# V's first projections in another order in the head of an attention and gated-MLP kernel

## The chip, the cores and the metric

The kernel runs on one NeuronCore of a Trainium2 chip. The metric is the device time of one execution in microseconds (us). A core has TensorE (PE; its weight loads are PEld), VectorE (DVE), ScalarE (ACT), GpSimd (POOL) and SyncE (SP); here SyncE mostly issues transfers.

## The reference, cut to what matters

x has 2048 rows of D = 640; all of it is bf16. There are 32 heads of 20, a causal window of W = 256, and an MLP of F = 1536.

```python
xn = layernorm(x)
q, k, v = split(xn @ wqkv)                 # 32 heads of 20
p = softmax(where(mask, q @ k.T * 20**-0.5, -1e9))   # 0 <= i - j < 256
a = (p @ v) @ wo
g, u = xn @ w_gate, xn @ w_up
out = x + a + (sigmoid(g) * u) @ w_down
```

## The kernel before, in words

The rows are worked off in four chunks of 512 (`NCH`, `CW`), each of four blocks of 128 rows (`SBC`). For a chunk the kernel needs xnT, the normalised rows transposed, so that D lies on the partitions as DC = 5 pieces of 128. Q and K are projected with the weights as the stationary operand (`proj_block`, L263), copied to bf16, written to a scratch in DRAM and read back spread over partitions. V is projected with xnT as the stationary operand, as it is wanted with rows on the partitions. Scores, softmax and the product with V are done in steps of up to eight pairs of 64-row blocks. Between these steps a planner (`class Fill`) pulls other PE work: the MLP's gate and up sums (`g_gu`, L411 and L420), the next chunk's projections, and the output. Its list is fixed when the program is built.

The change lies in the head, which does chunk 0 before the planner starts. Its order is written out by hand, and every engine carries out its own list in that order. PE transposes the normalised rows of a block itself (`transpose_rows`, L230: five transposes into a PSUM tile of the pool `ps_h`, then one or two copies to xnT at L231). The blocks come in the order 0, 1, 3, 2. Blocks 0 and 3 have their mean and variance from VectorE (`ln_half`, `ln_mv`, `norm`), blocks 1 and 2 from ScalarE (`mean_act`, `root_act`) with the last step on VectorE (`norm_act`, L647 and L648). V's sum of block s and half h (320 of 640 columns) is five matmuls, one for each piece of D (`project_v`, L301). It lies in a PSUM buffer of the pool `ps_d` (four buffers, taken in turn) or of `ps_h`. Two casts of 64 rows each bring it to the tile v (`copy_v`, L309).

Before the first transposes PE does ten matmuls on constant ones (L196), which nothing reads. All loads of the head go through SyncE's queue in the order written: block 0, 1 and 3 of x, the first half of V's weights (all five pieces, columns 0 to 319, 400 KB), block 2 of x, the other half of V's weights, Q's weights, K's weights (800 KB each), and the first quarters of w_gate and w_up (L156, 480 KB each). x's next chunk (L115) needs the buffer of chunk 0, so it is issued when all four blocks are normalised. After that GpSimd makes a small copy of it (`landed`, L700), which holds back two transfers that clear the scratch (L153). The Q and K projection of chunk 0 follows the head's last V sum on PE, and the planner's work follows that.

Of the kernel before, what the change touches and what calls it, by code (L numbers as in the profile page):

```python
# [9 lines left out]
P = 128  # L10
S = 2048
D = 640
# [3 lines left out]
DC = D // P  # L16
FC = F // P
CW = 512
# [6 lines left out]
HALF = 320  # L25
FS = 768
# [10 lines left out]
FP32 = mybir.dt.float32  # L37
# [29 lines left out]
def kernel(  # L67
# [11 lines left out]
    nc = tc.nc  # L79
# [23 lines left out]
    ps_h = banks.enter_context(tc.tile_pool(name="ps_h", bufs=4, space=bass.MemoryType.PSUM))  # L103
# [6 lines left out]
    def load_x(c):  # L110
        t = xp.tile([P, SBC, D], BF16, name="xc")
        xc[c] = t
        rows = x2[c * CW:(c + 1) * CW, :].rearrange("(a n t) d -> a t n d", a=SBC, n=SBC)
        for a in range(SBC):
            nc.sync.dma_start(out=t[32 * a:32 * a + 32], in_=rows[a])  # L115

    wqkv = const.tile([P, DC, 3 * D], BF16, name="wqkv")
    wqkv_r = A_wqkv.rearrange("(c p) n -> p c n", p=P)
    wg = [const.tile([P, DC, FS], BF16, name=f"wg{k}") for k in range(F // FS)]
    wu = [const.tile([P, DC, FS], BF16, name=f"wu{k}") for k in range(F // FS)]  # L120
# [3 lines left out]
    ones = nc.const_aps.tensor(1.0, [P, CW], BF16)  # L124
    def load_wqkv(part):
        nc.sync.dma_start(out=wqkv[:, :, part * D:(part + 1) * D],
                          in_=wqkv_r[:, :, part * D:(part + 1) * D])
# [3 lines left out]
    def load_rows(s, queue):  # L131
        queue.dma_start(out=xc[0][:, s, :], in_=xr[:, s, :])  # L132

    def load_v(hf):
        a = 2 * D + hf * HALF
        nc.sync.dma_start(out=wqkv[:, :, a:a + HALF], in_=wqkv_r[:, :, a:a + HALF])

    load_rows(0, nc.sync)
    load_rows(1, nc.sync)
    load_rows(3, nc.sync)  # L140
    load_v(0)
    load_rows(2, nc.sync)
    load_v(1)
    load_wqkv(0)
    load_wqkv(1)

# [8 lines left out]
    def load_gu(t, w, k, lo=0, hi=FS):  # L155
        nc.sync.dma_start(out=t[k][:, :, lo:hi],  # L156
                          in_=w.rearrange("(c p) f -> p c f", p=P)[:, :, k * FS + lo:k * FS + hi])

    load_gu(wg, B_w_gate, 0, 0, FS // 2)
    load_gu(wu, B_w_up, 0, 0, FS // 2)  # L160
    
    def load_second():
        load_gu(wg, B_w_gate, 1, FS // 2)
# [26 lines left out]
    nc.gpsimd.memset(eps, EPS)  # L190
    scr = const.tile([P, 1], FP32, name="scr")
    nc.scalar.activation(out=scr, in_=eps, func=SQRT)
    for n in (6, 4):
        ps = ps_d.tile([P, CW], FP32, name="pwarm", tag="d")
        for k in range(n):
            nc.tensor.matmul(ps, lhsT=ones[:, 0:P], rhs=ones, start=(k == 0), stop=(k == n - 1))  # L196


    xnT = {}
# [2 lines left out]
    def ln_half(c, s, a, stats=None):  # L202
        if a == 0:
            stats = lnp.tile([P, 2, nc.vector.BN_STATS_DIM], FP32, name="stats")
        nc.vector.bn_stats(out=stats[:, a, :], in_=xc[c][:, s, a * HALF:(a + 1) * HALF])
        return stats

    def ln_mv(stats, mv=None):
        if mv is None:
            mv = lnp.tile([P, nc.vector.BN_AGGR_DIM], FP32, name="mv")  # L210
        nc.vector.bn_aggr(out=mv, in_=stats)
        return mv
# [14 lines left out]
    def transpose_rows(s, copy, lo=0, hi=DC):  # L227
        pt = ps_h.tile([P, DC, P], BF16, name="pt", tag="pt")
        for d in range(lo, hi):
            nc.tensor.transpose(pt[:, d, :], xns[0, s][:, d * P:(d + 1) * P], ident)  # L230
        copy(out=xnT[0][:, s, lo:hi, :], in_=pt[:, lo:hi, :])  # L231
# [65 lines left out]
    def project_v(c, s, hf, lo=0, hi=DC, ps=None):  # L297
        if ps is None:
            ps = ps_d.tile([P, CW], FP32, name="pv", tag="d")
        for d in range(lo, hi):  # L300
            nc.tensor.matmul(ps[:, 0:HALF], lhsT=xnT[c][:, s, d, :],  # L301
                             rhs=wqkv[:, d, 2 * D + hf * HALF:2 * D + (hf + 1) * HALF],
                             start=(d == 0), stop=(d == DC - 1))
        return ps

    def copy_v(c, s, hf, ps, copy, blocks=(0, 1)):
        v4 = vt[c * SBC + s][:, :, 0:16 * VW].rearrange("p b (h d) -> p b h d", d=VW)
        for b in blocks:
            copy(out=v4[U * hf:U * hf + U, b, :, 0:DH],  # L309
                 in_=ps[U * b:U * b + U, 0:HALF].rearrange("p (h d) -> p h d", d=DH))  # L310

    def proj_v(c, s, hf, copy):
        copy_v(c, s, hf, project_v(c, s, hf), copy)
# [175 lines left out]
    def scores(c, step):  # L489
        pt = pp.tile([P, HG, NK, U], BF16, name="pT")  # L490
        ps = ps_s.tile([P, HG, CW], FP32, name="ps")
        for pr, k, q, n, col in step["pieces"]:
            kc, kb = divmod(c * NK + k, NK)
            half, r = divmod(pr, 2)
            for side in range(2):
                for i in range(HG):
                    nc.tensor.matmul(  # L497
                        ps[side * U:(side + 1) * U, i, col * U:(col + n) * U],
                        lhsT=qk["k", kc, half][32 * i:32 * i + DH, 2 * r + side, kb * U:(kb + 1) * U],
                        rhs=qk["q", c, half][32 * i:32 * i + DH, 2 * r + side, q * U:(q + n) * U],  # L500
                        start=True, stop=True)
        used = max(col + n for *_, n, col in step["pieces"])
        nc.scalar.activation(out=pt[:, :, 0:used, :], in_=ps[:, :, 0:used * U], func=EXP, scale=SCALE)  # L503

        if step["one"]:
            col, n, sign = step["one"]
            for side in range(2):
                select(pt[side * U:(side + 1) * U, :, col:col + n, :], n, sign)

        def masks():  # L510
            col, kind, n = step["pair"]
            part = pt[:, :, col:col + n, :].rearrange("p h n u -> p h (n u)")
            limit = keep[:, kind:kind + n, :].rearrange("p n u -> p (n u)").unsqueeze(1)
            nc.vector.tensor_tensor(out=part, in0=part, in1=limit.to_broadcast([P, HG, n * U]), op=MIN)  # L514

        return pt, masks
# [102 lines left out]
    def root(mv):  # L619
        r = lnp.tile([P, 1], FP32, name="rstd")  # L620
        nc.scalar.activation(out=r, in_=mv[:, 1:2], func=SQRT, bias=eps)
        return r
# [23 lines left out]
    def norm_act(s, xn, neg, r):  # L646
        nc.vector.reciprocal(r, r)  # L647
        nc.vector.tensor_scalar(out=xn, in0=xc[0][:, s, :], scalar1=neg[:, 0:1],  # L648
                                scalar2=r[:, 0:1], op0=ADD, op1=MULT)
# [10 lines left out]
    act, dve = nc.scalar.copy, nc.vector.tensor_copy  # L660
# [5 lines left out]
    stats3 = ln_half(0, 3, 0)  # L666
    for lo, hi in ((0, 3), (3, DC)):
        transpose_rows(0, act, lo, hi)
    norm_act(1, xn1, neg1, r1)
    mv3 = ln_mv(ln_half(0, 3, 1, stats3))  # L670
    transpose_rows(1, dve)
    v00 = project_v(0, 0, 0)
    r3 = root(mv3)
    xn2, neg2 = mean_act(2)
    r2 = root_act(2, xn2, neg2)
# [2 lines left out]
    copy_v(0, 0, 0, v00, dve, (0,))  # L678
    transpose_rows(3, dve)
    copy_v(0, 0, 0, v00, dve, (1,))  # L680
    v01 = project_v(0, 0, 1)
    norm_act(2, xn2, neg2, r2)
    copy_v(0, 1, 0, v10, act)
    v30 = project_v(0, 3, 0)
    copy_v(0, 0, 1, v01, act)
    v11 = project_v(0, 1, 1, ps=ps_h.tile([P, CW], FP32, name="pvh", tag="pt"))
    copy_v(0, 3, 0, v30, act)
    transpose_rows(2, dve)
    v31 = project_v(0, 3, 1, ps=ps_h.tile([P, CW], FP32, name="pvh", tag="pt"))
    copy_v(0, 1, 1, v11, act)  # L690
    copy_v(0, 3, 1, v31, dve)
    proj_v(0, 2, 0, act)
    proj_v(0, 2, 1, dve)
    nc.scalar.activation(out=scr, in_=neghalf[:, 0:1], func=EXP)
    banks.close()
    ps_s = banks.enter_context(tc.tile_pool(name="ps_s", bufs=1, space=bass.MemoryType.PSUM))
    load_x(1)
    load_gu(wg, B_w_gate, 0, FS // 2)
    landed = const.tile([P, 2], BF16, name="landed")
    nc.gpsimd.tensor_copy(out=landed, in_=xc[1][:, 0, 0:2])  # L700
# [55 lines left out]
    for t, (c, pr, k, step) in enumerate(todo):  # L756
# [10 lines left out]
        pt, masks = scores(c, step)  # L767
# [74 lines left out]
```

## Time and profile before

| | us |
|---|---|
| median of 3 runs | 309.64 |
| lowest and highest | 309.34 and 315.12 |
| the profiled execution's own time | 310.91 |
| its span, first to last instruction | 309.2 |
| V's first matmul in that execution | 7.01 |
| first Q/K matmul | 14.70 |
| first gate matmul (L411) | 25.49 |
| first up matmul (L420) | 26.57 |

Times within the profile count from the span's start. A row of a timeline has its start, its length, the engine, the line, the operation, the tiles written and read, the shape and the count; the length of several is from the first one's start to the last one's end. In square brackets is how long the engine had been idle and who ended that. A matmul's length has its drain in it, so back-to-back matmuls overlap. The chain of waits is followed back from the last instruction and shows start, length and who held the end; there the matmuls do not overlap, and their lengths are shares of the chain.

### The profile page before, as it was taken

Reading aid. Unit: us, or ns where it says so; the run is one execution under the profiler, and the core shown is the slowest. Engines: PE = TensorE matmul, PEld = TensorE weight load, DVE = VectorE, ACT = ScalarE, POOL = GpSimd, SP = SyncE. Lnnn points to the kernel's source line nnn. Section 1 sums busy time; section 2 is a strip of 40 time slices with the busy share of each in tenths; the row PEclk is TensorE's granted clock in tenths of the full one; section 3 lists DMA queues with packets and bytes.
Section 4 is the critical chain, followed back from the end, with each engine's and each line's share of the span. In section 5 each row is a group of like instructions: output and inputs, shape, how many; then the busy total and the mean of one; then the engine's idle time right before and its main releaser. Section 6 shows DMA issues by size and latency. Waiting matters only on the chain.

```text
span 309.2 us, 10136 instructions
## 1 busy us (share of the span) xinstructions
PE 305.0 (99%) x4431; PEld 169.0 (55%) x4431; DVE 186.3 (60%) x373; ACT 192.8 (62%) x184; POOL 83.8 (27%) x183
## 2 busy tenths in 40 slices
PE   8999999999999999999999999999999999999996
PEld 3654445564556655644456655654446665444774
DVE  4577548678992679577564557355383626465523
ACT  6823686888764657777674656877676466768000
POOL 5011124554314133332223132331313232231100
PEclk9999999999999999999999999999999999999999
DMA  7996939879937322540252112560000210000301
GB/s 213 344 265 192 346 90 274 226 239 310 211 125 176 119 73 87 174 137 11 78 127 63 47 58 88 167 203 2 2 2 3 66 45 23 2 2 2 87 22 64
DMA packets 35756, 36.86 MB, mean 119 GB/s; under 512 B 2944, under 2 KB 35456, under 8 KB 35712
## 3 DMA queue, kind: packets, MB, share of 16 engines
q1 hardware_dynamic: 34304, 33.84, 37.1%
q0 software_dynamic: 544, 1.61, 1.7%
q10 hardware_dynamic: 864, 0.77, 0.9%
q8 instruction: 34, 0.56, 0.8%
q14 instruction: 10, 0.08, 0.1%
HBM read 25.59 MB, written 11.44 MB: 120 GB/s over the span
## 4 chain that ended last, share of the span: by engine, by line
PE 97%; DMA 1%; ACT 1%; DVE 0%; SPq 0%; issue 0%
PE pg L411 18%; PE y L434 17%; PE pu L420 17%; PE pqk L263 14%; PE ps L497 9%; PE y L441 7%; PE acc L530 6%; PE pv L321 6%; PE pv L301 2%; DMA xc<-in_A_x_dram 1%; PE pt L230 0%; PE pvh L301 0%; ACT turn L637 0%; ACT turn L642 0%; DVE turn L648 0%; SPq L132 0%
## 5 line engine op out<-in xcount | busy, mean ns | idle before, releaser
L503 ACT ACTIVATE pT<-ps 128x2048 bf16<-128x2048 f32 x76 | 141.1, 1856 | 61.8 <-PE ps L497 56.2
L486 POOL TENSOR_SCALAR_AFFINE_SELECT pT<-pT 64x256 bf16<-64x256 bf16 (+1 forms) x120 | 67.7, 564 | 183.4 <-ACT pT L503 132.7
L411 PE MATMUL pg<-xnT,wg 128*128 128x512 bf16 x240 | 59.9, 380 | 0.0
L420 PE MATMUL pu<-xnT,wu 128*128 128x512 bf16 x240 | 59.8, 380 | 0.0
L424 DVE SCALAR_TENSOR_TENSOR h<-th,pu 128x512 bf16<-128x512 f32 x48 | 32.8, 683 | 44.4 <-ACT th L414 25.9
L434 PE MATMUL y<-wd,h 128*128 128x320 bf16 (+2 forms) x396 | 57.0, 296 | 0.0
L263 PE MATMUL pqk<-xnT,wqkv 128*128 128x512 bf16 x200 | 45.9, 381 | 0.0
L434 PEld LDWEIGHTS <-h 128*128 128x128 bf16 x396 | 36.7, 98 | 16.3 <-issue 2.5
L514 DVE TENSOR_TENSOR pT<-pT,keep 128x512 bf16<-128x512 bf16 (+1 forms) x76 | 35.3, 465 | 13.9 <-ACT pT L503 13.0
L414 ACT ACTIVATE th<-pg 128x512 f32<-128x512 f32 x48 | 28.6, 595 | 14.8 <-PE pg L411 14.3
L420 PEld LDWEIGHTS <-wu 128*128 128x128 bf16 x240 | 22.3, 98 | 27.6 <-issue 2.0
L411 PEld LDWEIGHTS <-wg 128*128 128x128 bf16 x240 | 21.7, 98 | 27.0 <-issue 3.6
L263 PEld LDWEIGHTS <-wqkv 128*128 128x128 bf16 x200 | 22.5, 119 | 19.2 <-issue 1.8
L497 PE MATMUL ps<-qT,kT 20*64 20x320 bf16 (+4 forms) x1440 | 32.2, 261 | 0.0
L445 DVE SCALAR_TENSOR_TENSOR rows<-y,rows 128x320 bf16<-128x320 f32 x30 | 14.6, 489 | 24.9 <-PE y L441 24.8
L541 DVE STREAM_TRANSPOSE t<-acc 128x512 f32<-128x512 f32 x32 | 20.9, 692 | 12.1 <-PE acc L530 12.1
L497 PEld LDWEIGHTS <-kT 20*64 20x64 bf16 x1440 | 13.1, 103 | 23.0 <-issue 21.9
L441 PE MATMUL y<-wo,oc 128*128 128x320 bf16 (+2 forms) x165 | 24.2, 295 | 0.0
L530 PEld LDWEIGHTS <-v 64*32 64x32 bf16 x1440 | 17.0, 92 | 6.7 <-issue 1.8
L530 PE MATMUL acc<-pT,v 64*32 64x320 bf16 (+4 forms) x1440 | 20.0, 253 | 0.0
L441 PEld LDWEIGHTS <-oc 128*128 128x128 bf16 x165 | 15.5, 98 | 6.5 <-issue 1.0
L321 PE MATMUL pv<-wqkv,xnT 128*64 128x320 bf16 x240 | 17.4, 300 | 0.0
(61 smaller groups left out, 177.4 us busy)
## 6 DMA issues: line engine op xcount, KB each, us to landing
qT<-sq SPq DMA_DIRECT2D x16, 256.0 KB, 4.6
kT<-sk SPq DMA_DIRECT2D x16, 256.0 KB, 5.0
xc<-in_A_x_dram SPq DMA_DIRECT2D x16, 160.0 KB, 4.0
sq<-st SPq DMA_DIRECT2D x20, 128.0 KB, 3.5
sk<-st SPq DMA_DIRECT2D x20, 128.0 KB, 2.6
out_dram<-rows SPq DMA_DIRECT2D x15, 160.0 KB, 1.8
wg<-in_B_w_gate_dram SPq DMA_DIRECT2D x4, 480.0 KB, 7.3
wu<-in_B_w_up_dram SPq DMA_DIRECT2D x4, 480.0 KB, 8.2
```

What stands on the lines that cost most here:

```text
L263: nc.tensor.matmul(ps, lhsT=wt[:, m, :], rhs=xnT[c][:, :, d, :], start=(d == 0), stop=(d == DC - 1))
L321: nc.tensor.matmul(ps[hf * U:(hf + 1) * U, 0:HALF], lhsT=xnT[c][:, s, d, rows], rhs=wqkv[:, d, 2 * D + hf * HALF:2 * D + (hf + 1) * HALF], ...
L411: nc.tensor.matmul(pg, lhsT=part(wg, d, f), rhs=xnT[c][:, :, d, :], start=(d == 0), stop=(d == DC - 1))
L420: nc.tensor.matmul(pu, lhsT=part(wu, d, f), rhs=xnT[c][:, :, d, :], start=(d == 0), stop=(d == DC - 1))
L424: nc.vector.scalar_tensor_tensor(out=h, in0=th, scalar=1.0, in1=pu, op0=ADD, op1=MULT)
L434: nc.tensor.matmul(y[:, 0:cut[1] - cut[0]], lhsT=ht[c, f][:, s * P:(s + 1) * P], rhs=wd[:, f, cut[0]:cut[1]], start=(f == 0), stop=False)
L441: nc.tensor.matmul(y[:, 0:cut[1] - cut[0]], lhsT=oc[c, m][:, s * P:(s + 1) * P], rhs=wo[:, m, cut[0]:cut[1]], start=False, stop=(m == DC - 1))
L486: nc.gpsimd.affine_select(out=part, in_=part, pattern=pattern, compare_op=GE, fill=0.0, base=-1 if sign > 0 else 0, channel_multiplier=sign)
L497: nc.tensor.matmul(ps[side * U:(side + 1) * U, i, col * U:(col + n) * U], lhsT=qk["k", kc, half][32 * i:32 * i + DH, 2 * r + side, kb * U: ...
L503: nc.scalar.activation(out=pt[:, :, 0:used, :], in_=ps[:, :, 0:used * U], func=EXP, scale=SCALE)
L514: nc.vector.tensor_tensor(out=part, in0=part, in1=limit.to_broadcast([P, HG, n * U]), op=MIN)
L530: nc.tensor.matmul(accs[side][32 * i:32 * i + 32, q * U:(q + n) * U], lhsT=vt[sb][rows, b, at:at + 32], rhs=pt[rows, i, col:col + n, :], s ...
```

## The change

V's weights are loaded by pieces of the contraction over all 640 columns: pieces 0 to 2 (480 KB) and pieces 3 and 4 (320 KB). On PE the first three matmuls of V's sum of block 0, half 0 stand between the transposes of block 0 and those of block 1, behind one more matmul on ones with 256 columns. Both halves of block 0 are summed ahead of block 1's first half, each in two parts; block 1's second half comes between the transposes of blocks 3 and 2. Casts change places between ScalarE and VectorE. The load of w_up's first quarter is issued behind x's next chunk.

```diff
-    def load_v(hf):
-        a = 2 * D + hf * HALF
-        nc.sync.dma_start(out=wqkv[:, :, a:a + HALF], in_=wqkv_r[:, :, a:a + HALF])
+    def load_v(lo, hi):
+        nc.sync.dma_start(out=wqkv[:, lo:hi, 2 * D:], in_=wqkv_r[:, lo:hi, 2 * D:])
...
-    load_v(0)
+    load_v(0, 3)
     load_rows(2, nc.sync)
-    load_v(1)
+    load_v(3, DC)
...
     load_gu(wg, B_w_gate, 0, 0, FS // 2)
-    load_gu(wu, B_w_up, 0, 0, FS // 2)
...
-    for n in (6, 4):
+    def warm(n, cols):
         ps = ps_d.tile([P, CW], FP32, name="pwarm", tag="d")
         for k in range(n):
-            nc.tensor.matmul(ps, lhsT=ones[:, 0:P], rhs=ones, start=(k == 0), stop=(k == n - 1))
+            nc.tensor.matmul(ps[:, 0:cols], lhsT=ones[:, 0:P], rhs=ones[:, 0:cols], start=(k == 0), stop=(k == n - 1))
+
+    warm(6, CW)
+    warm(4, CW)
...
     for lo, hi in ((0, 3), (3, DC)):
         transpose_rows(0, act, lo, hi)
+    warm(1, CW // 2)
+    v00 = project_v(0, 0, 0, 0, 3)
     norm_act(1, xn1, neg1, r1)
     mv3 = ln_mv(ln_half(0, 3, 1, stats3))
     transpose_rows(1, dve)
-    v00 = project_v(0, 0, 0)
+    v01 = project_v(0, 0, 1, 0, 3)
+    project_v(0, 0, 0, 3, DC, v00)
+    project_v(0, 0, 1, 3, DC, v01)
     r3 = root(mv3)
...
     transpose_rows(3, dve)
     copy_v(0, 0, 0, v00, dve, (1,))
-    v01 = project_v(0, 0, 1)
+    v11 = project_v(0, 1, 1)
     norm_act(2, xn2, neg2, r2)
+    copy_v(0, 0, 1, v01, act)
+    v30 = project_v(0, 3, 0, ps=ps_h.tile([P, CW], FP32, name="pvh", tag="pt"))
     copy_v(0, 1, 0, v10, act)
-    v30 = project_v(0, 3, 0)
-    copy_v(0, 0, 1, v01, act)
-    v11 = project_v(0, 1, 1, ps=ps_h.tile([P, CW], FP32, name="pvh", tag="pt"))
-    copy_v(0, 3, 0, v30, act)
     transpose_rows(2, dve)
     v31 = project_v(0, 3, 1, ps=ps_h.tile([P, CW], FP32, name="pvh", tag="pt"))
     copy_v(0, 1, 1, v11, act)
-    copy_v(0, 3, 1, v31, dve)
-    proj_v(0, 2, 0, act)
-    proj_v(0, 2, 1, dve)
+    copy_v(0, 3, 0, v30, dve)
+    copy_v(0, 3, 1, v31, act)
+    proj_v(0, 2, 0, dve)
+    proj_v(0, 2, 1, act)
...
     load_x(1)
+    load_gu(wu, B_w_up, 0, 0, FS // 2)
     load_gu(wg, B_w_gate, 0, FS // 2)
```

## The prediction

> **What bounds the kernel now.** I read the page's first two parts, then the chain of waits of the head, then the head's rows on PE, VectorE and SyncE's queue, and last the landing times of the loads.
>
> ```profile
> span 309.2 us, 10136 instructions
> ...
> PE 305.0 (99%) x4431; PEld 169.0 (55%) x4431; DVE 186.3 (60%) x373; ACT 192.8 (62%) x184; POOL 83.8 (27%) x183
> ```
>
> TensorE has work during 99% of the span and the chain that ended last lies on it for 97%. Behind the head comes one PE stream whose order the change leaves alone, so the time moves by as much as the first Q/K matmul (at 14.70 us) moves, unless a load comes late further on. The chain of waits of the head:
>
> ```profile
> 6.00 0.46 DVE turn L648
> 6.46 0.05 issue
> 6.50 0.71 PE pt L230 x5
> 7.22 2.67 PE pv L301 x10
> 9.88 0.46 PE pt L230 x5
> 10.35 1.44 PE pv L301 x10
> 11.79 0.68 PE pvh L301 x5
> 12.46 0.28 PE pt L230 x5
> 12.74 0.68 PE pvh L301 x5
> 13.42 1.44 PE pv L301 x10
> ```
>
> I call the five transposes of block s Ts, and V's sum of block s and half h Vsh. The order is T0, T1, V00, V10, T3, V01, V30, V11, T2, V31, V20, V21. A V matmul takes 2.67/10 = 0.267 us up to 9.9 and 0.68/5 = 0.136 after; five transposes take 0.53 and 0.28. So PE's rate doubles near 10.1, inside T3; the row PEclk reads full speed from the start, and the rate has to be taken from the matmuls. PE's own rows:
>
> ```profile
> 5.36 0.71 PE L230 MATMUL pt<-ident,turn 128*128 128x128 bf16 x5
> 6.50 0.71 PE L230 MATMUL pt<-ident,turn 128*128 128x128 bf16 x5 [0.43 <-DVE turn L648]
> 7.01 2.87 PE L301 MATMUL pv<-wqkv,xnT 128*128 128x320 bf16 x10
> 9.68 0.67 PE L230 MATMUL pt<-ident,turn 128*128 128x128 bf16 x5
> 10.18 1.60 PE L301 MATMUL pv<-wqkv,xnT 128*128 128x320 bf16 x10
> ```
>
> T0 is streamed by 5.36 + 5 x 0.107 = 5.90; T1 waits for block 1's normalised rows until 6.50. This 0.60 hole (0.43 from the end of the last result) is the only large one. VectorE between T3 and T2:
>
> ```profile
> 10.38 0.49 DVE L231 COPY xnT<-pt 128x640 bf16<-128x640 bf16 x1 [1.31 <-PE pt L230]
> 10.91 0.49 DVE L309 CAST v<-pv 64x320 bf16<-64x320 f32 x1
> 11.32 0.15 DVE L647 RECIPROCAL rstd<-rstd 128x1 f32<-128x1 f32 x1
> 11.51 0.45 DVE L648 TENSOR_SCALAR turn<-xc,neg,rstd 128x640 bf16<-128x640 bf16 x1
> ```
>
> T2 needs the last of these: 11.96, and 0.05 to issue, 12.01. PE came to T2 at 12.30, so this chain had 0.29 to spare, and no more.
>
> **The change, part by part.** Times on this execution's clock.
>
> *V00's first part before T1.* T0 ends its stream at 5.90; the added 256-column matmul takes half of a warm-up matmul (ten started from 0.85 to 4.64, 0.42 each), 0.21, to 6.11. It lies in the hole; without the hole it would cost its 0.21. V00 over chunks 0 to 2 needs two things. ScalarE's copy of chunks 0 to 2 runs from 5.90 to 6.38. The weights: before, the first V load was issued at 2.19 and landed 4.1 later, at 6.3; now it carries 480 KB instead of 400, in runs of 1280 bytes instead of 640. Per engine that is 24 packets for 40; I take the same landing, 6.3. Bounds: before 6.38 nothing is gained, as the copy ends then; late, block 2's rows, issued behind it, landed at 2.67 + 4.0 = 6.7. So it starts at 6.50, bounds 6.45 and 6.77. T1 was ready at 6.50, and is now queued behind three matmuls of 0.267: it starts at 7.30. What waits for T1: VectorE's copy (now 8.07 to 8.56), then block 3's norm (7.85 + 0.45 before, now to 9.23), then T3, which PE reaches at 10.58. These 0.80 are not lost, as V00 is three matmuls shorter later. This edit costs 0, bounds -0.05 and +0.27.
>
> *V01 ahead of V10.* After T1 (to 7.83) come three matmuls of V01 to 8.63, two of V00 to 9.17, two of V01 to 9.70, then V10. The second weight load is needed at 8.63. Its landing has no row; it lies between block 2's rows, 6.7, and Q's weights, 3.71 + 6.8 = 10.5. Q's 800 KB should take what K's took, 12.8 - 10.5 = 2.3, so V's old 400 KB were there by 8.2, and the new 320 KB by about 6.7 + 0.8 x 1.5 = 7.9 (estimate). Cost 0; the late end, 8.2, is also in time. With the clock doubling at 10.1, V10 ends at 10.58 and T3's stream at 10.86. Before, T3's ended at 10.18 with three V sums still to come before T2; now two, V11 and V30.
>
> *Two sums instead of three between T3 and T2.* T3's stream end to T2 ready was 12.01 - 10.18 = 1.83, all on VectorE and in an unchanged order (copy, cast, reciprocal, norm). Before, PE filled it with 3 x 0.68 and a 0.07 wait for the copy of T3, 2.11. Now it has 2 x 0.68 + 0.07 = 1.43. The stall is 1.83 - 1.43 = 0.40, before T2. So T2 starts at 10.86 + 1.83 = 12.69 against 12.30. Bounds: 0, if T3 got as much earlier as VectorE then needs; and 0.68, a whole sum, if the spare 0.29 vanished as well. I take 0.40, as all its terms are rows of this very chain.
>
> *Copies shared anew.* ScalarE still makes ten half casts (0.86 a pair) and VectorE six. V21's cast moves to ScalarE and V20's to VectorE; the PSUM buffer of V21 is wanted by the fourth Q/K sum, 3 x 1.08 after the first, and its cast is done 1.1 after V21. ScalarE's table load (1.28) then ends some 0.5 later, while its next work was at 21.38. Cost 0. T2 to Q/K stays 14.70 - 12.30 = 2.40.
>
> *w_up's first quarter, 480 KB, moved.* It leaves SyncE's row at 6.31 (2.02 of issuing) and goes behind the four loads of x's second chunk and ahead of a w_gate quarter and ten Q/K stores. x's loads wait for block 2's norm, now 12.64, and take 1.76 of issuing; w_up and w_gate 0.43 each end at about 15.4, and the first store waits for VectorE until 17.1. The bytes before the stores are the same. x lands about 480 KB, or 1.5 us, earlier; w_up then lands after x at 17 to 19, where its first user was at 26.57. GpSimd's clearing transfers wait for x (19.59 before) and start 3 earlier: 768 KB more beside w_up and w_gate, 2.2 at the 344 or so GB/s of the page's second slice. Even with all of that w_up is there by 21. Cost 0, cover 5 us or more; an up-weight later than 26.6 would cost its lateness.
>
> **Sum:** 0 + 0 + 0.40 + 0 + 0 = +0.40 on the profiled execution's 310.91 us (span 309.2, 1.7 around it), so 311.3. The median of the runs shown, 309.64, is 1.27 lower. An execution whose rate doubled before T0 would fit: with fast matmuls T1 stays at 6.50, V00 at 6.78, V10 waits for T1's copy to 7.67, T3 8.35 to 8.63, then V01, V30, V11 end at 10.75, and Q/K starts at 10.75 + 2.40 = 13.15, 1.55 less. In that case the change gives: V00's first part 6.37, T1 6.78, V01's first part 7.06, V00's rest waits for the second load from 7.47 to some 7.77, T3 ends at 9.27, T2 at 11.10, Q/K at 13.50: +0.35. Either way about +0.4; on the median **310.0 us**.
>
> [...]
>
> **The rivals.**
> A, faster: the rate doubles at 6.7, because PE's hole shrinks from 0.60 to 0.39 and sums stand on both sides of T1. It decides on whether these 0.21 are enough for the hole not to count. Then T1 is at 7.04, V00's rest at 7.8, V10 at 8.27, T3 ends at 9.23, T2 starts at 11.06, Q/K at 13.46: -1.24, 308.4 on the median. For it: the hole lies 3.6 us ahead of the doubling, and the median run fits an early doubling. Against: 0.85 to 5.3 had no hole, and the rate did not double.
> B, the weights gate T1: the larger first load lands with block 2's rows at 6.7, V00 starts at 6.77 and all behind it with it: +0.27 more, +0.67, 310.3. For it: 80 KB more ahead of its end. Against: 24 packets an engine for 40.
> C, neutral: T3 comes early enough, or VectorE's chain is short enough, that the stall is covered: 0, 309.6. Against: the chain has 0.29 of slack and loses a cover of 0.68.
> D, slower: the second weight load lands after 8.63, say at 8.9, PE gets a hole there, and the doubling comes 3.6 behind it, at 12.5. Then V10 ends at 11.30, T3's stream at 11.83, and T2 starts 1.83 later, at 13.7: +1.4, 311.0. It decides at a landing of 8.63. For it: this landing has no row. Against: 7.9 by the bytes, and at the latest 8.2.
>
> **How the numbers follow.** The forecast's chance is 0.5, A 0.14, B 0.12, C 0.12, D 0.09, and 0.03 for a late load or a disturbance of 2% (6.2 us, about what a measurement of this kernel can tell from no change: its runs lay between 309.34 and 315.12). The range runs from A, 308.3, past D to the forecast from the profiled execution's own time, 311.3 with 0.1 to spare; the forecast's own is 309.7 to 310.4. All five cases are within 2%: faster 0.01, same 0.96, slower 0.03.
>
> **What would show it.** In the changed profile: V00's first matmul at 6.4 to 6.8 and T1 behind it at 7.2 to 7.6 on the slow clock; no wait before V00's rest; PE idle 0.3 to 0.5 before T2, put down to VectorE's norm; x's loads landed near 17; first Q/K matmul 0.4 later than in the same clock state. A matmul rate that doubles before 9 us in the changed kernel's record would not by itself make the forecast wrong, as executions may differ in it; what would is PE reaching T2 after the norm, a second hole before V00's rest on the slow clock, or a load that PE waits for behind the head.

## The result, and the profile after

| | before | changed |
|---|---|---|
| median of 18 runs | 309.4 us | 311.25 us |
| lowest and highest | 309.15 and 315.12 | 310.0 and 313.74 |
| ratio to before | | 1.0061, 95% interval 1.0043 to 1.0078 |
| the profiled execution's time, span | 310.91, 309.2 | 310.0, 308.3 |
| first Q/K matmul in it | 14.70 | 13.81 |

The changed kernel is slower by 0.6%, clear of noise and inside 2%. Another series of runs (r_after below), beside its own executions of before, gave 310.31 against 309.49 (ratio 1.0029, 0.9996 to 1.0062), an interval that just reaches 1. The single profile seems to say the opposite: the changed kernel's span is 0.9 shorter. That is the state of PE's clock in the two executions. The page of the profile after:

```profile
span 308.3 us, 10137 instructions
...
PE 303.7 (99%) x4432; PEld 168.2 (55%) x4432; DVE 186.3 (60%) x373; ACT 192.7 (62%) x184; POOL 84.4 (27%) x183
```

PE's rows of the changed head:

```profile
5.31 0.72 PE L231 MATMUL pt<-ident,turn 128*128 128x128 bf16 x5
5.82 0.42 PE L194 MATMUL pwarm<-const-bfloat16-1.0 128*128 128x256 bf16 x1
6.82 0.57 PE L302 MATMUL pv<-wqkv,xnT 128*128 128x320 bf16 x3 [0.58 <-DMA wqkv<-in_A_wqkv_dram]
7.22 0.44 PE L231 MATMUL pt<-ident,turn 128*128 128x128 bf16 x5
7.50 1.96 PE L302 MATMUL pv<-wqkv,xnT 128*128 128x320 bf16 x12
9.30 0.44 PE L231 MATMUL pt<-ident,turn 128*128 128x128 bf16 x5
9.58 0.84 PE L302 MATMUL pv<-wqkv,xnT 128*128 128x320 bf16 x5
10.33 0.85 PE L302 MATMUL pvh<-wqkv,xnT 128*128 128x320 bf16 x5
11.40 0.45 PE L231 MATMUL pt<-ident,turn 128*128 128x128 bf16 x5 [0.22 <-DVE turn L649]
```

Five transposes take 0.72 at 5.31 and 0.44 at 7.22: the rate doubled between 6.0 and 6.8 here, and at 10.1 in the profile of before. So the two profiles can't be subtracted. What can be compared is each wait: PE stood before V00 for the weights (a wait that before did not have) and before T2 for block 2's norm. Behind the head nothing changed: from the first Q/K matmul to the end it is 309.21 - 14.70 = 294.51 before and 308.30 - 13.81 = 294.49 after. In twelve of the thirteen profiles of this document it lies between 294.4 and 294.9; the thirteenth, of e_v00a, comes at the end.

The comparable profile of before is that of e_wu below: PE's list is that of before, its rate doubled ahead of T0, and its Q/K projection begins at 13.24 in an execution of 309.46. Against it the changed kernel's profiled execution lost 0.57 in the head and 310.0 - 309.46 = 0.54 in time.

### The profile page after: what moved, and what is told of

It reads as the page before. It is cut to its first block, busy times and chain, and to the rows that moved or that the text cites. A ratio compares the mean times of both kernels' runs of the same rounds, so it can differ in the third digit from the quotient of the medians.

```text
span 308.3 us, 10137 instructions
## 1 busy us (share of the span) xinstructions
PE 303.7 (99%) x4432; PEld 168.2 (55%) x4432; DVE 186.3 (60%) x373; ACT 192.7 (62%) x184; POOL 84.4 (27%) x183
## 4 chain that ended last, share of the span: by engine, by line
PE 96%; ACT 1%; DVE 1%; DMA 1%; issue 0%; SPq 0%
PE pg L412 18%; PE y L435 18%; PE pu L421 17%; PE pqk L264 15%; PE ps L498 9%; PE y L442 7%; PE acc L531 6%; PE pv L322 6%; PE pv L302 1%; DMA xc<-in_A_x_dram 1%; ACT turn L638 1%; DVE turn L649 0%; ACT turn L643 0%; PE pt L231 0%; PE pvh L302 0%
## 5 line engine op out<-in xcount | busy, mean ns | idle before, releaser
L415 ACT ACTIVATE th<-pg 128x512 f32<-128x512 f32 x48 | 28.5, 595 | 14.7 <-PE pg L412 14.3
```

## The experiments

In the tables "low clock" counts executions whose mean granted clock was 0.997 or less. One stretch of 3.4 us at half rate, as e_nowarm's profile below shows it from 7.4 to 10.8, is 1.7 of 310 us; that execution reads 0.994. Before had 4 of 109 such executions in the four series of the experiments; the changed kernel had 9 of 30, counting the 18 executions of its result and the 12 of r_after. The kernels of one series were run beside the same executions of before; each of the four series ran on another chip, so counts and medians of different series are compared with care.

| first series (before 309.49) | median | fastest | ratio, interval | low clock |
|---|---|---|---|---|
| r_after | 310.31 | 309.74 | 1.0029, 0.9996 to 1.0062 | 4 of 12 |
| e_wu | 309.50 | 309.18 | 0.9981, 0.9954 to 1.0007 | 1 of 12 |
| e_nowu | 310.39 | 309.70 | 1.0015, 0.9987 to 1.0043 | 2 of 12 |
| e_v10 | 310.42 | 309.62 | 1.0019, 0.9991 to 1.0048 | 4 of 12 |

**r_after**: the changed kernel again.

> The changed kernel again, for a second profile. Theory 1 (clock): the changed head has three holes on PE (before V00, before V00's rest, before T2), which cost some 0.65 us in an execution whose matmul rate doubles by 6.8 us, and beyond that they make the rate double later or fall back in a part of the executions, 1.7 us for each stretch of 3.4 at half rate; so times from 310.0 to 313, median 311.2, and a profile that either looks like the first one or shows V's matmuls at 0.267 us past 7 us. Theory 2 (queue): the moved load of w_up puts later transfers in each other's way, and PE waits somewhere behind 14 us; the same times, but the profile shows a wait of PE behind the head.

The profile looked like the first: V00 at 6.71, the first Q/K matmul at 13.71, no wait behind the head. The times fell into three heaps, 309.74 to 310.02, 310.6 to 310.68 and 312.01 to 312.73; the last heap is the four with a low clock. Nothing for theory 2. The median that theory 1 gave, 311.2, was missed.

**e_wu**: before, with only the moved load of w_up.

```diff
     load_gu(wg, B_w_gate, 0, 0, FS // 2)
-    load_gu(wu, B_w_up, 0, 0, FS // 2)
...
     load_x(1)
+    load_gu(wu, B_w_up, 0, 0, FS // 2)
     load_gu(wg, B_w_gate, 0, FS // 2)
```

> The kernel before with the load of w_up's first quarter alone moved behind x's next chunk. Theory 1 (clock): the PE order and its holes are those of before, so 309.4 within 0.2, with a spread as narrow as before's. Theory 2 (queue): 310.5 to 311.3 with the wide spread.

309.50, as before: the move costs nothing. Its rows on PE:

```profile
5.37 0.45 PE L229 MATMUL pt<-ident,turn 128*128 128x128 bf16 x5 [0.75 <-DVE turn L223]
6.51 0.45 PE L229 MATMUL pt<-ident,turn 128*128 128x128 bf16 x5 [0.69 <-DVE turn L647]
6.80 1.60 PE L300 MATMUL pv<-wqkv,xnT 128*128 128x320 bf16 x10
8.24 0.44 PE L229 MATMUL pt<-ident,turn 128*128 128x128 bf16 x5
8.79 1.53 PE L300 MATMUL pv<-wqkv,xnT 128*128 128x320 bf16 x10
...
13.24 1.03 PE L262 MATMUL pqk<-xnT,wqkv 128*128 128x512 bf16 x4
```

This is before's order with the early clock: T1 at 6.51, right behind it V00 at 6.80, and only one small wait later, 8.52 to 8.79, for the second half of V's weights.

**e_nowu**: the reverse, the changed kernel with that load at its old place.

> The changed kernel with the load of w_up's first quarter at its old place. Theory 1 (clock): 311.0 to 311.4, spread from 310 to 313, as PE's holes stay. Theory 2 (queue): 309.8 to 310.1 with a narrow spread.

310.39 beside r_after's 310.31: the load is not the cause. The forecast of 311.0 to 311.4 took the median of the result for the whole, and missed.

**e_v10**: the changed kernel with V10 behind T3.

```diff
-    v10 = project_v(0, 1, 0)
     copy_v(0, 0, 0, v00, dve, (0,))
     transpose_rows(3, dve)
     copy_v(0, 0, 0, v00, dve, (1,))
+    v10 = project_v(0, 1, 0)
     v11 = project_v(0, 1, 1)
```

> The changed kernel with V10 moved from ahead of T3 to behind it, so that three V sums lie between T3 and T2 again, as before. Theory 1 (clock): the hole before T2 is gone, 0.2 to 0.4 less than the changed kernel in the same clock state, and fewer executions at half rate if that hole is one of those that matter: 310.3 to 311.0. Theory 2 (queue): 0.2 to 0.4 less from the head and the same spread as the changed kernel.

```profile
6.74 0.57 PE L302 MATMUL pv<-wqkv,xnT 128*128 128x320 bf16 x3 [0.85 <-DMA wqkv<-in_A_wqkv_dram]
...
11.05 0.44 PE L231 MATMUL pt<-ident,turn 128*128 128x128 bf16 x5
...
13.45 0.81 PE L264 MATMUL pqk<-xnT,wqkv 128*128 128x512 bf16 x3
```

T2 has no wait, and the Q/K projection begins at 13.45 against 13.71 in r_after, whose V00 began within 0.03 of it: the stall before T2 is worth 0.26. The low clocks stayed (4 of 12), so they do not need that stall.

| second series (before 309.46) | median | fastest | ratio, interval | low clock |
|---|---|---|---|---|
| e_fill | 310.55 | 309.80 | 1.0027, 1.0009 to 1.0044 | 0 of 12 |
| e_nowarm | 311.82 | 309.98 | 1.0049, 1.0028 to 1.0071 | 5 of 11 |
| e_v00a | 310.17 | 309.56 | 1.0027, 1.0007 to 1.0047 | 1 of 12 |
| e_bfill | 309.55 | 309.12 | 0.9993, 0.9967 to 1.0019 | 0 of 12 |

**e_nowarm**: the changed kernel without the line `warm(1, CW // 2)`.

> The changed kernel without the added matmul on ones behind T0, so the hole before V00 is 0.1 to 0.2 us longer. Theory 1a: executions with a mean clock near 0.995 are as frequent as in the changed kernel or more, 4 to 8 in 12, median 310.5 to 312. Theory 1b: 3 or 4 in 12. In both the fastest stay at 309.7 to 310.0, as the matmul lies in the hole.

This profile caught the clock falling back. PE's rows, and the granted clock in three stretches of it (columns: stretch, length, busy time and count of PE, PEld, DVE, ACT, POOL, then PEclk, DMA share, GB/s):

```profile
5.36 0.45 PE L231 MATMUL pt<-ident,turn 128*128 128x128 bf16 x5 [0.64 <-DVE turn L225]
7.10 0.68 PE L302 MATMUL pv<-wqkv,xnT 128*128 128x320 bf16 x3 [1.29 <-DMA wqkv<-in_A_wqkv_dram]
7.57 0.74 PE L231 MATMUL pt<-ident,turn 128*128 128x128 bf16 x5
8.11 3.14 PE L302 MATMUL pv<-wqkv,xnT 128*128 128x320 bf16 x12
11.08 0.44 PE L231 MATMUL pt<-ident,turn 128*128 128x128 bf16 x5
```

```profile
4.10:7.40 3.30, 1.37 (x11) 0.70 (x10) 2.43 (x8) 2.63 (x9) 0.56 (x3) 1.00 0.99 328
7.50:10.80 3.30, 3.30 (x18) 2.08 (x16) 1.49 (x4) 2.59 (x7) 0.00 (x0) 0.50 1.05 379
10.90:14.30 3.40, 3.17 (x29) 1.95 (x28) 2.12 (x6) 1.85 (x5) 0.00 (x0) 1.00 0.70 217
```

T0 takes 0.45, T1 0.74, T3 0.44: PE was fast, then slow, then fast. The clock is full to 7.4, halved to 10.8 and full again, though PE was busy all through the slow stretch. What went before it is a stretch in which PE had 1.37 of work in 3.30, with a hole of 1.29 from the last result to V00, waiting for V's weights. The Q/K projection begins at 15.60, 1.89 later than in r_after; 0.39 of that is V00's later start (7.10 against 6.71), so the slow stretch itself cost about 1.5.

**e_fill**: two matmuls of 512 columns in place of the one of 256 (`warm(2, CW)`).

> The changed kernel with two 512-column matmuls on ones behind T0 in place of the one of 256 columns, so that PE is idle for 0.65 us or less before V00 in place of about 1.0. Theory 1a (the hole before V00 closes the clock gate again in a part of the executions, mean clock 0.995 there): such executions become as rare as in the kernel before, at most 1 in 12, the fastest stay at 309.7 to 310.0, and the median falls to 309.9 to 310.1. Theory 1b (the short holes behind V00 close it): as often as in the changed kernel, 3 or 4 in 12, median 310.4 to 311.2.

No low clock in 12, against 9 of 30 and 5 of 11: theory 1a's count. The median did not fall to the forecast 309.9 to 310.1, though: 310.55. In its profile the first load landed 5.1 after its issue, V00 began at 7.29 and Q/K at 14.31. So the clock's falling back isn't all that separates the executions; the landing of the load is another part.

**e_v00a**: before with its loads by halves, and only V00's first three matmuls ahead of T1.

```diff
     for lo, hi in ((0, 3), (3, DC)):
         transpose_rows(0, act, lo, hi)
+    v00 = project_v(0, 0, 0, 0, 3)
...
     transpose_rows(1, dve)
-    v00 = project_v(0, 0, 0)
+    project_v(0, 0, 0, 3, DC, v00)
```

> The kernel before with its loads by halves, and only the first three matmuls of V00 moved ahead of T1; no added matmul. If the larger first load is what delays V00 and with it T1 (landing 6.7 to 6.9 in the changed kernel, 6.3 before), V00 starts at 6.4 here and the cost is 0 to 0.3: fastest 309.2 to 309.5. If the place of V00 ahead of T1 costs by itself: 309.6 or more for the fastest. Theory 1a: the hole is 0.75 to 0.9, as before, so a mean clock near 0.995 in at most 1 of 12; theory 1b the same.

```profile
6.76 0.57 PE L301 MATMUL pv<-wqkv,xnT 128*128 128x320 bf16 x3 [0.99 <-DMA wqkv<-in_A_wqkv_dram]
...
8.19 0.85 PE L301 MATMUL pv<-wqkv,xnT 128*128 128x320 bf16 x5 [0.31 <-DVE xnT L231]
...
13.67 3.62 PE L263 MATMUL pqk<-xnT,wqkv 128*128 128x512 bf16 x16
```

The 400 KB landed 4.5 after the issue, as the 480 KB did in three profiles, and V00 began at 6.76, not 6.4. T1 follows it, so V10 waits for T1's copy until 8.19, and Q/K begins at 13.67, 0.43 later than in e_wu. The fastest, 309.56, lies between the two forecasts; the median is 310.17. The rows decide: the place ahead of T1 costs by itself, and not because the load grew.

**e_bfill**: before with three matmuls on ones of 256 columns behind T0.

> The kernel before with three added matmuls on ones of 256 columns behind T0, which fill its hole before T1 in part. Theory 1a: the executions of before at 310.2 to 311.2, which double their rate late, become fewer: median 309.2 to 309.4, fastest unchanged at 309.15. If the hole of before does not matter to the clock: the same spread as before beside it.

309.55 beside 309.46, where 309.2 to 309.4 was forecast. The highest was 310.3, where before had 6 of 34 above that, which points to its late executions being thinned out; twelve runs do not show it.

| third series (before 309.31); e_chunk: fourth (before 309.58) | median | fastest | ratio, interval | low clock |
|---|---|---|---|---|
| e_t1 | 310.46 | 309.64 | 1.0030, 1.0016 to 1.0045 | 0 of 12 |
| e_t1v10 | 310.05 | 309.04 | 1.0019, 1.0004 to 1.0035 | 1 of 12 |
| e_chunk | 310.68 | 310.09 | 1.0052, 1.0030 to 1.0073 | 5 of 12 |

**e_t1**: the changed kernel with T1 ahead of V00 again; **e_t1v10**: that, and V10 behind T3.

```diff
     warm(1, CW // 2)
-    v00 = project_v(0, 0, 0, 0, 3)
...
     transpose_rows(1, dve)
+    v00 = project_v(0, 0, 0, 0, 3)
     v01 = project_v(0, 0, 1, 0, 3)
```

> The changed kernel with T1 ahead of V00's first three matmuls again, all else as changed. Theory (the wait for the first weight load, moved ahead of T1, makes one hole of the two and closes the clock gate): T1 starts at 6.5 and cuts the hole, so a mean clock near 0.995 in at most 1 of 12; the first Q/K matmul some 0.1 earlier than in the changed kernel in the same state (the stall before T2 stays), fastest 309.6 to 309.9, median 309.8 to 310.2. Rival (the clock closes by the later holes, before V00's rest and before T2): 3 to 4 of 12, median 310.4 to 311.2.

> The changed kernel with T1 ahead of V00's first three matmuls and V10 behind T3; the chunked loads, V01 ahead of V10, the casts and w_up's load stay as changed. Theory: with the two orders undone nothing of the loss is left: first Q/K matmul at 13.2 to 13.4, fastest 309.1 to 309.4, median within 0.2 of the kernel before. Rival (the chunked loads or the casts cost something of their own): fastest 309.6 or more.

With T1 back at 6.51 no execution of e_t1 had a low clock, as the theory said; but the median, 310.46, is the rival's. e_t1v10 has a run at 309.04, as fast as before's fastest, and yet a median 0.7 above before's. Its profile shows why, in the chain of waits:

```profile
3.19 5.81 DMA wqkv<-in_A_wqkv_dram
9.00 0.04 issue
```

and in PE's rows:

```profile
6.51 0.45 PE L231 MATMUL pt<-ident,turn 128*128 128x128 bf16 x5 [0.58 <-DVE turn L649]
7.73 0.97 PE L302 MATMUL pv<-wqkv,xnT 128*128 128x320 bf16 x6 [0.77 <-DMA wqkv<-in_A_wqkv_dram]
9.04 0.70 PE L302 MATMUL pv<-wqkv,xnT 128*128 128x320 bf16 x4 [0.34 <-DMA wqkv<-in_A_wqkv_dram]
```

In this execution the first load landed 5.5 after its issue and the second 5.8, at 9.0. With pieces of the contraction every sum needs both. Theory and rival were both half right, and the loads' cut was still to be tried alone.

**e_chunk**: before with V's weights loaded by pieces of the contraction, nothing else (the two `load_v` edits of the change).

> The kernel before with V's weights loaded by pieces of the contraction and nothing else. Theory (every sum now needs both loads, so V00's fourth matmul, at 7.2 us where the clock is full, waits for the second load, which landed at 7.6 to 9.0 in the runs so far; before, that load is first needed behind T3): a wait of PE inside V00 for the load, first Q/K matmul 0.4 to 1.0 later than 13.2, median 309.8 to 310.4. Rival (the loads' cut is neutral and only the orders on PE cost): no wait inside V00, median within 0.2 of the kernel before.

```profile
6.72 0.57 PE L300 MATMUL pv<-wqkv,xnT 128*128 128x320 bf16 x3
7.94 1.11 PE L300 MATMUL pv<-wqkv,xnT 128*128 128x320 bf16 x7 [0.65 <-DMA wqkv<-in_A_wqkv_dram]
...
13.68 0.59 PE L262 MATMUL pqk<-xnT,wqkv 128*128 128x512 bf16 x2
```

V00 stops after three matmuls and waits for the second load until 7.94; Q/K begins at 13.68, 0.44 later than in e_wu, and 5 of 12 executions had a low clock. This one edit gives 1.1 us of median (ratio 1.0030 to 1.0073), above the 309.8 to 310.4 of its forecast. The whole change gave 1.85 and 0.8, each in another series, so the medians do not rank the two. The heads can be compared: with the first load landing 4.5 after its issue in both, Q/K begins at 13.68 here and at 13.71 in r_after. In these two profiles the changed order on PE is, as a whole, neither a gain nor a loss on top of the loads by pieces: V01's first part bridges most of the second wait, while V00 ahead of T1 moves the first wait to where it holds T1, and the stall before T2 comes on top.

## Why the prediction was right or wrong, point by point

The measured 311.25 lies inside 308.3 to 311.4 and on the forecast's side, but the forecast itself, +0.4, was too small: +1.85 in the result and +0.8 in the series after it. That the median lies inside is partly luck: the upper end was +0.4 on an execution whose rate doubled late, at 10.1, while the sum holds neither the late landings nor the fall of the clock that the runs show. With the same clock the sum came closer: +0.35 computed, 0.57 between the profiles of e_wu and of the changed kernel.

*V00's first part before T1, "costs 0, bounds -0.05 and +0.27": this step failed.* It took the first load's landing, 4.1 after the issue, from the one profile there was. (Its own terms, a landing at 6.3 and a copy that ends at 6.38, give a start near 6.4 and not the 6.50 that it writes, and block 3's norm would end near 9.1, not 9.23; neither changes the sum.) In thirteen profiles the first V load landed 4.1 to 5.5 after its issue: with 400 KB 4.1, 4.6, 4.5 and 5.1, with 480 KB 4.6, 4.5, 4.7, 4.5, 5.1, 4.9, 4.1, 5.5 and 4.5. The size, which rival B was built on, makes no difference that these few profiles show; the spread does, and 4.1 was its short end. Before, T1 stood ahead of this wait and V00 could start at 6.80 (e_wu), so that a landing up to 6.8 cost nothing. In the changed kernel every tenth of a late landing past 6.4 holds V00, T1 and all behind them. In r_after, the first profile, e_nowu and e_fill V00 began at 6.71, 6.82, 6.93 and 7.29, and Q/K at 13.71, 13.81, 13.90 and 14.31: the delay is passed on whole, and the late bound of the step, 6.77, was exceeded in three of the four. Computed for an early clock were 6.37 and 13.50. So B's wait came about, though not by B's reason, and e_v00a shows that this place alone costs 0.43 in the head.

*V01 ahead of V10, "cost 0; the late end, 8.2, is also in time".* This was right for a slow clock and a landing by 8.63; e_t1v10's came at 9.0. With the early clock, which twelve of the thirteen profiles had, PE was ready for V00's rest at 7.9 and waited for the second load (issued at 3.19, landed 4.8 later) to 8.08; in e_t1v10 to 9.04. The prediction's own sum for an early clock has this wait, from 7.47 to 7.77, but its list of costs has 0. The price sat in the edit to the loads, which that list treated only as a size: alone, it costs 0.44 in the head (e_chunk).

*The stall before T2, 0.40.* The mechanism is shown: the norm ends at 10.90 + 0.45 = 11.35, T2 starts at 11.40. From T3's stream end, 9.58, that is 1.82 against the 1.83 computed, and PE's stream was empty from 11.02 (its last sum, 10.33, a gap of 0.01 and five matmuls of 0.136), so for 0.38. Undone, it gave back only 0.26 (e_v10), since T3 then waits at 8.72 for block 3's norm.

*Copies and w_up's load, cost 0.* e_wu and e_nowu show the load's move to cost nothing. The landing of x's next chunk was foreseen wrongly (GpSimd's copy that waits for it came at 18.7, not near 17), under cover that was wide enough. The casts weren't tried alone; no row of PE's in the head waits for one in the profiles.

*The clock.* The reading that the runs of before had an early clock, unlike their profile, held: e_wu's first Q/K matmul was at 13.24 against 13.15 computed. Rival A, 308.4, is out: the fastest execution of the changed kernel took 309.74. That a smaller hole brings the doubling to 6.7, A's condition, no run shows: the first profile of the changed kernel doubled between 6.0 and 6.8, but e_wu's, with PE's list of before, ran T0 at the full rate (0.45) at 5.37. C, neutral, is out as well, since PE waits before T2 in both profiles of the changed kernel. D came nearest, with a chance of 0.09: a hole, and behind it a stretch at half rate. But what the runs show is not a later doubling, it is a fall back to half for one stretch (3.4 us in e_nowarm), with a low clock in 9 of 30 executions. e_nowarm shows it happening, at a cost of about 1.5 in the head. That emptiness of PE is the cause rests on counts and is not shown. For it: 5 of 11 without the fill, 5 of 12 with a second hole (e_chunk), 0 of 12 with a longer fill, 0 and 1 of 12 with T1 between and the fill kept (e_t1, e_t1v10). Against the length of the hole before V00 alone: e_v00a has no fill, a hole of 0.99 in its profile, and 1 of 12. The loads by pieces go with the low clocks too: kernels with the loads by halves had 6 in 145 executions, those with the loads by pieces 26 in 113, of which e_fill, e_t1 and e_t1v10 had 1 in 36. Twelve executions of a kernel are few; of the low clocks only e_nowarm's profile shows where in the kernel the stretch lies.

What stays open: how the 1.85 of the result divides among executions, since the changed kernel gave +0.8 in the next series; and why e_fill's median did not fall although its low clocks went. Without its five executions of low clock the result's median would be 310.62, still 1.2 above before's, and the head of the profiled one explains 0.57. The landing of the load varies enough to do much of the rest. So does the time at which the rate first doubles, which the mean clock does not show: the profile of before, with its doubling at 10.1, reads 1.000 and took 1.45 more than e_wu's. Neither is known for an execution that was not profiled.

## What to carry to other kernels

A transfer that is waited for behind other ready work has slack; the same wait moved ahead of that work has none, and then its spread over executions counts (here 4.1 to 5.5 from issue to landing), not its time in one profile; in e_v00a the place alone cost 0.43 in the head. Cutting a weight load along the contraction makes every sum need all parts, cutting it by output columns lets the first sums go with the first part; the difference was 0.44 in the head (e_chunk against e_wu). In a head, an empty stretch on PE may cost more than its length: in e_nowarm the clock was halved for 3.4 us behind one of 1.29, for about 1.5 us of time.

## What the runs showed of the hardware that was not expected

In e_nowarm's profile the full clock was lost again within the head; in e_v00a's a stretch with little work did not lose it. In e_nowarm PE had 1.37 of work in the 3.30 us from 4.1; the granted clock read 0.50 in the 3.30 from 7.5, in which PE was busy for 3.30, and 1.00 from 10.9 on to 14.3. In e_v00a PE had 2.08 of work in the 3.40 from 5.3, and the clock read 1.00 there and in the 3.40 from 8.7, with ten of V's matmuls in 1.44 from 9.32. In the profile of before V's matmuls were slow, 0.267 each, through a stretch that was full: PE was busy for 2.45 of the 3.30 us from 0, 2.88 of the 3.40 from 3.3 and 3.40 of the 3.40 from 6.7, and the rate doubled at 10.1 (the clock reads 1.00 in all of these, so the rate is that of the matmuls). What decides it, the work in a stretch, the length of one hole or something else, these profiles do not show.

Once, in e_v00a, PE stood for 1.37 us at 82.84 with no releaser in the profile, and the execution was 1.6 longer behind the head than the others, most of it this stop. It was in one of thirteen profiles.
